# Attention and a three-way maxout layer on one core: raw weights decoded three in a row in the middle of a visit

## The chip, the cores and the metric

One core of a Trainium2 chip runs the whole program. The metric is the time of one execution on the device in microseconds, as the median of several runs.

## The reference, cut to what matters

```python
# q, k, v: (8, 12, 448, 64) float32
scores = q @ k.T / sqrt(64) - log(448)
attn   = 1 / (1 + exp(-scores))
x      = (attn @ v), heads side by side        # 3584 tokens x 768
h      = max(x @ w1, x @ w2, x @ w3)           # each weight 768 x 768
out    = h @ w_out                             # 768 x 768
```

The weights reach the kernel as the bits of float64 numbers, two 32-bit words each, and the kernel turns them into float32 itself: that is a "decoding".

## The kernel before, in words

Every product of two float32 matrices is made of three matmuls on a high and a low part of each operand (`hi` is the operand rounded, `lo` is what is left: ScalarE copies `hi`, VectorE subtracts). The attention part takes the first 246 us. Behind it come twelve visits: three stages of four visits, one for each pair of batches, and a stage is one block of output columns. In a visit a 2x2 block product by Winograd's scheme needs seven block products (`PRODUCTS`) for each of the three weights: 21 products of nine matmuls. In the texts they are counted @0 to @20: @0 to @6 are w1 (q = 0), @7 to @13 w2, @14 to @20 w3. Then the last layer runs 15 steps for each of the four pairs (`STEPS`, two output halves a step, six matmuls each).

Order: every instruction is pinned, so each engine and SP's DMA queue run in program order, and a wait holds all that stands behind it. The order inside a visit is: the product's matmuls; what takes its result; the copies and subtractions for the next visit's tokens (`his`, `los`, mostly at @14 to @20 and at the first products of the next visit); the splits of the next stage's weights (`ws`); weight loads (`w_loads`); then a decoding, if the list `decodes` names this place.

What takes the results: the first product of a weight goes to PSUM bank 0, and ScalarE copies it (`p1`, L807); the second goes to bank 1 and VectorE adds `p1` (`u2`, L810); the third to bank 3, VectorE adds `u2` (`u3`, L813); the fourth to bank 2, and `put("22")` adds `u3` (L786 for w1, L791 and the maximum L792 for w2 and w3). The fifth goes on in bank 0, the sixth takes a new buffer of bank 1, the seventh goes on in bank 2 after `put("22")` has read it (`put("12")`). Banks 2 and 3 have one buffer, 0 and 1 have two.

A decoding (`decode`, L203 to L225) is two ScalarE activations (L210, L211) and four VectorE instructions (L212 to L221) on a tile `wb`, of which there is one. Stage weights are then stored to DRAM (L238); the last layer's go into tiles `wd0` to `wd2`, and after every third `l_sums` puts fifteen sums of them into the tile `sums` on GpSimd (L264), with stores that follow over the next twelve products. The generator loads `ahead` raw tiles (`wraw`): at a decoding it first issues the load of the tile `ahead - 1` further on, then decodes, then stores.

Other users of the queues: at the head of a visit `x_load_all` issues seven loads of the next visit's tokens on SP (stages 1 and 2); in stage 0 the tokens are loaded at @4 and GpSimd forms their sums (L314, twelve instructions). `w_load` loads four blocks of the next stage's weights (L178) and GpSimd forms four sums (L173). In the last visit (`plan`, `EARLY`) the last layer's first operands are loaded (`l_load`), summed on GpSimd (`l_sum`, L648), copied (`l_hi`, L662, with a second copy into PSUM at L665) and subtracted (`l_lo`, L672), and its weights are split likewise (`wl_split`, L686 and L688; `wl_lo`, L695). All PSUM copies share one pair of banks (`ps_av`).

Of the kernel before, what the change touches and what calls it, by code (L numbers as in the profile page):

```python
# [8 lines left out]
F32 = mybir.dt.float32  # L9
F32R = mybir.dt.float32r  # L10
# [3 lines left out]
ALU = mybir.AluOpType  # L14
# [3 lines left out]
P = 128  # L18
# [21 lines left out]
L_SUMS = (  # L40
    ("n9", "a6", "+", "a7"),
    ("w3", "a1", "-", "n9"),
    ("w8", "w3", "-", "a8"),
    ("n12", "a5", "+", "w8"),
    ("w10", "a2", "+", "n12"),
    ("n16", "a4", "+", "a8"),
    ("w6", "n9", "+", "n16"),
    ("w9", "a5", "-", "a6"),
# [48 lines left out]
def attention_then_maxout(  # L97
# [9 lines left out]
    nc = tc.nc  # L107
    B, NK = qk.shape[0], qk.shape[1]
    S = qk.shape[3] // 2
    T = B * S  # L110
    C = S // P
    HALF = NK // 2
# [3 lines left out]
    pin = tc.keep_in_program_order  # L116
# [21 lines left out]
    xo_p = [pool(ctx, "xo", 1)]  # L138
# [111 lines left out]
    wl, wl_p, w_work = [], [], []  # L250
# [89 lines left out]
    FIRST = [x for _, x, _ in PRODUCTS[:2]]  # L340
# [239 lines left out]
    c_p = pool(ctx, "c", 2, reuse_waits="tile")  # L580
    dec_p = pool(ctx, "dec2", 1, reuse_waits="tile")
# [18 lines left out]
    his, los, ws, w_loads = {}, {}, {}, {}  # L600

    for n in range(1, done):
        (st0, p0), (st, p) = visits[n - 1], visits[n]
        if st != st0:
            when = [[(n - 1, 1, k // 2) for k in range(7)],
                    [(n - 1, 2, 2 + k // 2) for k in range(7)],
                    [(n, 0, 3 + k // 2) for k in range(6)] + [(n, 1, 0)]]
            for q in range(3):
                for key, (name, _, _) in zip(when[q], PRODUCTS):
                    ws.setdefault(key, []).append((q, name))  # L610
            w_loads[n - 2, 0, 0] = st, 0
            w_loads[when[0][-1]] = st, 1
            w_loads[when[1][-1]] = st, 2
        if p != p0:
            for k, (_, name, _) in enumerate(PRODUCTS):
                his[n - 1, 2, k] = name
            keys = [(n - 1, 2, k) for k in range(1, 5)] + [(n, 0, k) for k in (0, 2, 3)]
            for key, (_, name, _) in zip(keys, PRODUCTS):
                los[key] = name
# [5 lines left out]
    BEFORE = 3 * len(PRODUCTS)  # L625
    slots = ["xs_b11", "xs_t2", "xs_b12", "xs_t1", "xs_b21", "xs_t4", "xs_b22"]
    SETS = ("b11", "t2", "t3", "t1")
    l_raw, l_ops, l_px, wl_ops = {}, {}, {}, {}
# [26 lines left out]

    def l_hi(v, s):
        g, x = v * len(STEPS) + s, l_raw[v, STEPS[s][1]][0]
        name = SETS[g % len(SETS)]
        to = xo_p[name not in FIRST]
        hi = to.tile([P, HALF, S], F32R, name=f"xhi_{name}")  # L660
        lo = to.tile([P, HALF, S], F32R, name=f"xlo_{name}")
        pin(nc.scalar.copy(out=hi[:, :2], in_=x))  # L662
        if room(v, s):
            px = ps_av.tile([P, 2, 512], F32, name="ps_av")
            pin(nc.scalar.copy(out=px[:, :, :S], in_=x))  # L665
            x = px[:, :, :S]
        l_ops[g], l_px[g] = (hi, lo), x

    def l_lo(v, s):
        g = v * len(STEPS) + s  # L670
        hi, lo = l_ops[g]
        pin(nc.vector.tensor_tensor(  # L672
            out=lo[:, :2], in0=l_px.pop(g), in1=hi[:, :2].bitcast(F32), op=ALU.subtract
        ))

    def wl_load(j):
# [23 lines left out]
    for v in pairs:  # L700
# [6 lines left out]

    EARLY = {
        (l_load, "b3"): 4, (l_load, "b1"): 4, (l_load, "b2"): 5, (l_load, "b0"): 6,
        (l_load, "b5"): 7, (l_load, "b4"): 16,  # L710
        (l_sum, "s7"): 8, (l_sum, "s2"): 9, (l_sum, "s3"): 10, (l_sum, "s0"): 12,
        (l_sum, "s6"): 19, (l_sum, "s15"): 20,
        (l_hi, 0): 16, (l_hi, 1): 18, (l_hi, 2): 19, (l_hi, 3): 20,
        (l_lo, 0): 17, (l_lo, 1): 19, (l_lo, 2): 20, (l_lo, 3): 21,
    }

    def place(v, s, _, run, what, *rest):
# [20 lines left out]
    for j in range(2 * len(STEPS) * 2 // HALF):  # L738
        plan.setdefault(j + 1, []).append(lambda j=j: wl_load(j))
    for at, *tiles in (  # L740
        *((2 * k + 5, 2 * k, 2 * k + 1) for k in range(7)),
        (BEFORE, 14, 15), (BEFORE + 1, 16), (BEFORE + 4, 17), (BEFORE + 6, 18), (BEFORE + 7, 19),
    ):
        made = []
        plan.setdefault(at, []).append(lambda made=made, tiles=tiles: made.extend(wl_split(*tiles)))
        plan.setdefault(at + 1, []).insert(0, lambda made=made: wl_lo(*made))

    def l_plan(at):
# [1 line left out]
            run()  # L750

    decodes = {
        0: (8, 14), 1: (6, 10, 14), 2: (6, 10, 14), 3: (10,), 4: (0, 6, 10, 13), 5: (10, 13),
        6: (4, 10, 13), 8: (0, 10, 13), 9: (4, 10, 13), 10: (4,),
    }
    decodes = [(n, *divmod(at, len(PRODUCTS))) for n in decodes for at in decodes[n]]
    todo = [(1, 2, 3)] + [(2, q, n) for q in range(3) for n in range(4)]
    todo += [(STAGES, u, n) for u in range(2) for n in range(2 * HALF)]
    background = decoding(dec_p, todo, 1, 2, c_p)


    x_first = xs
# [107 lines left out]
    def l_out(q, name):  # L870
        to, tag, bufs = {
            "c": ((c_p, "p1", 1), (c_p, "u2", 1)),
            "t": ((m_p, "m11", 1), (m_p, "m22", 1)),
            "u": ((m_p, "m12", 1), (m_p, "m21", 1)),
            "d": ((c_p, "u3", 1), (c_p, "c", 2)),
            "e": ((wl_p[0], "e", 1), (c_p, "c", 2)),
        }[name][q]
        return to.tile([P, S], F32, name=tag, bufs=bufs)

# [90 lines left out]
```

## Time and profile before

| | |
|---|---|
| median of 3 runs | 868.73 us (867.54 to 872.42) |
| the profiled execution | 871.16 us, span from first to last instruction 869.3 us |
| TensorE busy | 850.3 us, 98% |
| VectorE, ScalarE, GpSimd busy | 77%, 55%, 26% |
| HBM | 113.31 MB read, 52.69 MB written |
| busy DMA queues | hardware ones, q1 with 165.92 of 166.95 MB |

A row of the timeline has the start and the length in us, the engine, the line, the operation and its operands; a bracket says how long the engine stood idle before it and what released it. Busy shares are averages over stages with different limits.

### The profile page before, as it was taken

The page shows a single profiled execution, that of the slowest core. Times are in us where ns is not written, and L with a number is a line of the kernel's source. Part 1 is how long each engine was busy: PE and PEld are TensorE (multiplying, and loading weights), DVE is VectorE, ACT ScalarE, POOL GpSimd, SP SyncE. Part 2 cuts the span into 40 slices and gives each one's busy share as a digit, 9 for nine tenths or more (in the row PEclk, how much of TensorE's full clock was granted, in tenths as well). Part 3 has the DMA queues.
Part 4 walks back from the last instruction along what each step waited for, and adds up shares of the span by engine and source line. Part 5 has one row for each costly group of instructions (what it writes and reads, how often), then busy time and mean ns, then how long its engine had stood idle before and what let it go on. Part 6 is the DMA issues. An engine that isn't in the chain of part 4 may idle for free.

```text
span 869.3 us, 14523 instructions
## 1 busy us (share of the span) xinstructions
PE 850.3 (98%) x5410; PEld 701.6 (81%) x5410; DVE 669.5 (77%) x928; ACT 479.2 (55%) x654; POOL 230.3 (26%) x192
## 2 busy tenths in 40 slices
PE   9999999999999999999899989999999998999998
PEld 5555555555579989899799978999989997999997
DVE  5677668876888897977586768769595778897895
ACT  6888888888864251423243333135152468777774
POOL 0010020202115436212000050250303227677660
PEclk9999999999999999999999999999999999999999
DMA  8667776776684656524643741292834643645423
GB/s 290 206 208 242 250 252 231 259 278 227 207 305 186 203 197 230 206 61 170 230 168 146 269 132 43 71 348 81 304 133 177 224 131 125 206 139 206 139 74 127
DMA packets 79878, 166.95 MB, mean 192 GB/s; under 512 B 7616, under 2 KB 55744, under 8 KB 79808
## 3 DMA queue, kind: packets, MB, share of 16 engines
q1 hardware_dynamic: 79664, 165.92, 54.9%
q8 instruction: 42, 0.69, 0.3%
q14 instruction: 28, 0.23, 0.1%
q10 hardware_dynamic: 144, 0.11, 0.0%
HBM read 113.31 MB, written 52.69 MB: 191 GB/s over the span
## 4 chain that ended last, share of the span: by engine, by line
PE 85%; DVE 4%; DMA 4%; issue 3%; POOL 2%; SPq 1%; ACT 0%; DVEq 0%; POOLq 0%; ACTq 0%
PE ps_y L591 42%; PE ps_y L860 16%; PE ps_s L430 9%; PE ps_s L454 7%; PE ps_av L454 6%; PE ps_s L465 2%; PE ps_s L443 2%; PE ps_av L430 2%; DMA wraw<-w 1%; DMA ws_a<-w_dram 1%; DVE c L791 1%; POOL sums L264 1%; DVE wb L216 1%; DVE wb L220 1%; DVE wb L212 0%
## 5 line engine op out<-in xcount | busy, mean ns | idle before, releaser
L400 ACT ACTIVATE a<-ps_s,bias_s 128x896 f32<-128x896 f32 x121 | 114.7, 1017 | 10.8 <-PE ps_s L430 10.7
L591 PE MATMUL ps_y<-xhi_t,wlo_s 128*128 128x448 f32 x324 | 117.3, 362 | 2.9 <-DVE c L791 2.9
L591 PE MATMUL ps_y<-xhi_t,whi_s 128*128 128x448 f32 x324 | 117.4, 362 | 0.0
L591 PE MATMUL ps_y<-xlo_t,whi_s 128*128 128x448 f32 x324 | 117.3, 362 | 0.0
L173 POOL TENSOR_TENSOR ws_s<-ws_a,ws_a 128x384 f32<-128x384 f32 x9 | 10.0, 1116 | 312.3 <-DMA ws_a<-w_dram 206.5
L807 ACT COPY p<-ps_y 128x448 f32<-128x448 f32 x36 | 19.1, 532 | 125.2 <-PE ps_y L591 104.3
L591 PE MATMUL ps_y<-xhi_b,wlo_a 128*128 128x448 f32 x216 | 78.6, 364 | 2.8 <-ACT p L807 2.8
L591 PE MATMUL ps_y<-xhi_b,whi_a 128*128 128x448 f32 x216 | 78.7, 364 | 0.0
L591 PE MATMUL ps_y<-xlo_b,whi_a 128*128 128x448 f32 x216 | 78.5, 363 | 0.0
L210 ACT ACTIVATE c<-wraw 128x384 f32<-128x384 f32 x48 | 27.5, 572 | 74.1 <-DVE m L792 38.3
L591 PEld LDWEIGHTS ps_y<-xhi_t,wlo_s 128*128 128x128 f32 x324 | 60.7, 187 | 7.5 <-DVE c L791 3.5
L591 PEld LDWEIGHTS ps_y<-xlo_t,whi_s 128*128 128x128 f32 x324 | 60.8, 188 | 4.3
L591 PEld LDWEIGHTS ps_y<-xhi_t,whi_s 128*128 128x128 f32 x324 | 60.8, 188 | 3.8
L454 PE MATMUL ps_av<-a,v 64*64 64x448 f32 x576 | 62.6, 536 | 0.0
L454 PE MATMUL ps_s<-a,v 64*64 64x448 f32 x576 | 59.7, 544 | 0.0
L791 DVE TENSOR_TENSOR c<-ps_y,u 128x448 f32<-128x448 f32 x72 | 44.5, 619 | 14.7 <-PE ps_y L591 14.4
L412 DVE TENSOR_TENSOR lo<-qk,hi 128x896 fp32r<-128x896 f32 (+4 forms) x51 | 53.5, 1049 | 1.8
L792 DVE TENSOR_TENSOR m<-c,m 128x448 f32<-128x448 f32 x72 | 52.8, 733 | 2.5
L454 PEld LDWEIGHTS ps_av<-a,v 64*64 64x64 f32 x576 | 22.0, 133 | 32.1 <-issue 32.1
L430 PE MATMUL ps_s<-hi 64*128 64x448 f32 x240 | 47.0, 388 | 0.0
L349 DVE TENSOR_TENSOR xlo_b<-xs_b,xhi_b 128x1344 fp32r<-128x1344 f32 x30 | 46.8, 1560 | 0.0
L349 DVE TENSOR_TENSOR xlo_t<-xs_t,xhi_t 128x1344 fp32r<-128x1344 f32 x30 | 46.5, 1549 | 0.0
(204 smaller groups left out, 2229.6 us busy)
## 6 DMA issues: line engine op xcount, KB each, us to landing
qk<-qk SPq DMA_DIRECT2D x47, 448.0 KB, 4.7
xs_b<-x_dram SPq DMA_DIRECT2D x30, 672.0 KB, 7.6
wraw<-w SPq DMA_DIRECT2D x36, 384.0 KB, 5.4
xs_t<-t_dram SPq DMA_DIRECT2D x18, 672.0 KB, 8.1
v<-v SPq DMA_DIRECT2D x24, 448.0 KB, 5.7
h_dram<-m SPq DMA_DIRECT2D x48, 224.0 KB, 1.9
x_dram<-m SPq DMA_DIRECT2D x47, 224.0 KB, 3.0
t_dram<-xs_t SPq DMA_DIRECT2D x12, 672.0 KB, 4.6
```

What stands on the lines that cost most here:

```text
L210: pin(nc.scalar.activation(out=square, in_=high.bitcast(F32), func=AF.Square))
L349: pin(nc.vector.tensor_tensor(out=lo, in0=x, in1=hi.bitcast(F32), op=ALU.subtract))
L400: pin(nc.scalar.activation(out=a, in_=banks[:, :, :S], func=AF.Sigmoid, bias=bias_s, scale=scale))
L412: pin(nc.vector.tensor_tensor(out=lo[:, cols], in0=t[:, cols], in1=high.bitcast(F32), op=ALU.subtract))
L430: pin(nc.tensor.matmul(bank[e][:, :S], kt[r, S + c * P : S + (c + 1) * P], qt[r, :S], start=n == 0, stop=n == len(terms) - 1,))
L443: pin(nc.tensor.matmul(ps[g * D : (g + 1) * D, e, :S], t[r, S + C * P :], t[r, :S], start=True, stop=True,))
L454: pin(nc.tensor.matmul(ps[e * D : (e + 1) * D, :S], vt[rows, (g * C + c) * 2 + e], chunks[c][rows, e], start=c == 0 and not (ahead and r = ...
L591: pin(nc.tensor.matmul(ps[:, :S], wt[:, k * P : (k + 1) * P], xt[:, k], start=first and n == 0, stop=n == len(terms) - 1, skip_group_check ...
L791: pin(nc.vector.tensor_tensor(out=c, in0=y, in1=add, op=ALU.add))
L792: pin(nc.vector.tensor_tensor(out=m[name], in0=c, in1=m[name], op=ALU.max))
L807: pin(nc.scalar.copy(out=p1, in_=ps[0][:, :S]))
L860: pin(nc.tensor.matmul(ps[:, :S], wl_ops[j][part][:, c * P : (c + 1) * P], xt[:, k], start=first and m == 0, stop=m == len(terms) - 1, ski ...
```

## The change: what it does

The places of the decodings move (`decodes`): from up to four in a visit, at places from @0 to @14, to mostly three in a visit at @4, @6 and @8. `ahead` goes from 2 to 3. The first weight load of the last stage moves from visit 6 @0 to @9. In the last visit the first operand of the last layer gets its high and low part in the tile `sums`, so that it can be split at @11 and not @16; the next three go to the sets of tiles that come free, at @15, @17 and @19; the sums and the weight splits move accordingly, and two more weight splits are done singly, without the copy into PSUM. For the space, the tile `e` goes (its place is `sums`), and a scratch area is halved.

```diff
--- before.py
+++ after.py
@@ -608,7 +608,7 @@
             for q in range(3):
                 for key, (name, _, _) in zip(when[q], PRODUCTS):
                     ws.setdefault(key, []).append((q, name))
-            w_loads[n - 2, 0, 0] = st, 0
+            w_loads[(n - 2, 0, 0) if st == 1 else (n - 2, 1, 2)] = st, 0
             w_loads[when[0][-1]] = st, 1
             w_loads[when[1][-1]] = st, 2
         if p != p0:
@@ -655,11 +655,19 @@
 
     def l_hi(v, s):
         g, x = v * len(STEPS) + s, l_raw[v, STEPS[s][1]][0]
-        name = SETS[g % len(SETS)]
-        to = xo_p[name not in FIRST]
-        hi = to.tile([P, HALF, S], F32R, name=f"xhi_{name}")
-        lo = to.tile([P, HALF, S], F32R, name=f"xlo_{name}")
-        pin(nc.scalar.copy(out=hi[:, :2], in_=x))
+        if g:
+            name = SETS[(g - 1) % len(SETS)]
+            to = xo_p[name not in FIRST]
+            hi, lo = (
+                to.tile([P, HALF, S], F32R, name=f"x{part}_{name}")[:, :2] for part in ("hi", "lo")
+            )
+        else:
+            both = wl_p[0].tile([P, len(L_SUMS) * P], F32R, name="sums")
+            hi, lo = (
+                both[:, k * 2 * S : (k + 1) * 2 * S].rearrange("p (a s) -> p a s", a=2)
+                for k in range(2)
+            )
+        pin(nc.scalar.copy(out=hi, in_=x))
         if room(v, s):
             px = ps_av.tile([P, 2, 512], F32, name="ps_av")
             pin(nc.scalar.copy(out=px[:, :, :S], in_=x))
@@ -670,7 +678,7 @@
         g = v * len(STEPS) + s
         hi, lo = l_ops[g]
         pin(nc.vector.tensor_tensor(
-            out=lo[:, :2], in0=l_px.pop(g), in1=hi[:, :2].bitcast(F32), op=ALU.subtract
+            out=lo, in0=l_px.pop(g), in1=hi.bitcast(F32), op=ALU.subtract
         ))
 
     def wl_load(j):
@@ -707,11 +715,11 @@
 
     EARLY = {
         (l_load, "b3"): 4, (l_load, "b1"): 4, (l_load, "b2"): 5, (l_load, "b0"): 6,
-        (l_load, "b5"): 7, (l_load, "b4"): 16,
-        (l_sum, "s7"): 8, (l_sum, "s2"): 9, (l_sum, "s3"): 10, (l_sum, "s0"): 12,
-        (l_sum, "s6"): 19, (l_sum, "s15"): 20,
-        (l_hi, 0): 16, (l_hi, 1): 18, (l_hi, 2): 19, (l_hi, 3): 20,
-        (l_lo, 0): 17, (l_lo, 1): 19, (l_lo, 2): 20, (l_lo, 3): 21,
+        (l_load, "b5"): 7, (l_load, "b4"): 12,
+        (l_sum, "s7"): 8, (l_sum, "s0"): 9, (l_sum, "s2"): 10, (l_sum, "s3"): 11,
+        (l_sum, "s6"): 17, (l_sum, "s15"): 19,
+        (l_hi, 0): 11, (l_hi, 1): 15, (l_hi, 2): 17, (l_hi, 3): 19,
+        (l_lo, 0): 12, (l_lo, 1): 16, (l_lo, 2): 18, (l_lo, 3): 20,
     }
 
     def place(v, s, _, run, what, *rest):
@@ -738,8 +746,9 @@
     for j in range(2 * len(STEPS) * 2 // HALF):
         plan.setdefault(j + 1, []).append(lambda j=j: wl_load(j))
     for at, *tiles in (
-        *((2 * k + 5, 2 * k, 2 * k + 1) for k in range(7)),
-        (BEFORE, 14, 15), (BEFORE + 1, 16), (BEFORE + 4, 17), (BEFORE + 6, 18), (BEFORE + 7, 19),
+        *((at, 2 * k, 2 * k + 1) for k, at in enumerate((5, 7, 9, 12, 14, 16, 18))),
+        (BEFORE + 1, 14), (BEFORE + 4, 15), (BEFORE + 6, 16), (BEFORE + 7, 17), (BEFORE + 8, 18),
+        (BEFORE + 9, 19),
     ):
         made = []
         plan.setdefault(at, []).append(lambda made=made, tiles=tiles: made.extend(wl_split(*tiles)))
@@ -750,13 +759,13 @@
             run()
 
     decodes = {
-        0: (8, 14), 1: (6, 10, 14), 2: (6, 10, 14), 3: (10,), 4: (0, 6, 10, 13), 5: (10, 13),
-        6: (4, 10, 13), 8: (0, 10, 13), 9: (4, 10, 13), 10: (4,),
+        0: (8,), 1: (6, 9), 2: (8,), 3: (4, 6, 8), 4: (0, 5, 8), 5: (4, 6, 8),
+        6: (4, 6, 8), 8: (4, 6, 8), 9: (4, 6, 8), 10: (4, 6, 8),
     }
     decodes = [(n, *divmod(at, len(PRODUCTS))) for n in decodes for at in decodes[n]]
     todo = [(1, 2, 3)] + [(2, q, n) for q in range(3) for n in range(4)]
     todo += [(STAGES, u, n) for u in range(2) for n in range(2 * HALF)]
-    background = decoding(dec_p, todo, 1, 2, c_p)
+    background = decoding(dec_p, todo, 1, 3, c_p)
 
 
     x_first = xs
@@ -873,7 +882,7 @@
             "t": ((m_p, "m11", 1), (m_p, "m22", 1)),
             "u": ((m_p, "m12", 1), (m_p, "m21", 1)),
             "d": ((c_p, "u3", 1), (c_p, "c", 2)),
-            "e": ((wl_p[0], "e", 1), (c_p, "c", 2)),
+            "e": ((wl_p[0], "sums", 1), (c_p, "c", 2)),
         }[name][q]
         return to.tile([P, S], F32, name=tag, bufs=bufs)
 
@@ -956,7 +965,7 @@
         "wout": by_tiles(moe_w_out),
     }
     nc = bacc.Bacc(
-        "TRN2", target_bir_lowering=False, num_devices=1, dynamic_dma_scratch_size=2048
+        "TRN2", target_bir_lowering=False, num_devices=1, dynamic_dma_scratch_size=1024
     )
     args = [
         nc.dram_tensor(name, a.shape, mybir.dt.from_np(a.dtype), kind="ExternalInput").ap()
```

## Rows read from the trace of the kernel before

**Rows 1.** The page: busy time by engine; one of the costliest groups.

```profile
PE 850.3 (98%) x5410; PEld 701.6 (81%) x5410; DVE 669.5 (77%) x928; ACT 479.2 (55%) x654; POOL 230.3 (26%) x192
...
L791 DVE TENSOR_TENSOR c<-ps_y,u 128x448 f32<-128x448 f32 x72 | 44.5, 619 | 14.7 <-PE ps_y L591 14.4
```

**Rows 2.** Timeline of TensorE from 246 us on, the matmuls that waited.

```profile
320.90 0.47 PE L591 MATMUL ps_y<-xhi_b,wlo_s 128*128 128x448 f32 x1 [0.97 <-DVE c L791]
...
361.29 0.57 PE L591 MATMUL ps_y<-xhi_b,wlo_s 128*128 128x448 f32 x1 [1.97 <-DVE c L791]
...
425.32 0.47 PE L591 MATMUL ps_y<-xhi_b,wlo_a 128*128 128x448 f32 x1 [2.76 <-ACT p L807]
...
516.46 0.47 PE L591 MATMUL ps_y<-xhi_t,wlo_s 128*128 128x448 f32 x1 [2.87 <-DVE c L791]
...
523.86 0.47 PE L591 MATMUL ps_y<-xhi_b,wlo_s 128*128 128x448 f32 x1 [1.72 <-DVE c L791]
...
638.34 0.47 PE L591 MATMUL ps_y<-xhi_b,wlo_s 128*128 128x448 f32 x1 [0.79 <-DVE c L791]
...
718.93 0.47 PE L860 MATMUL ps_y<-xlo_t,whi_s 128*128 128x448 f32 x1 [0.31 <-DVE xlo_t L672]
...
726.37 0.47 PE L860 MATMUL ps_y<-xhi_t,wlo_a 128*128 128x448 f32 x1 [2.52 <-DVE p L903]
```

**Rows 3.** Span and mean granted TensorE clock of the core.

```profile
core 0: 869.3 us, clock 0.994
```

**Rows 4.** Windows behind two waits: length, busy us (count) by engine, clock, DMA share, GB/s.

```profile
361.30:364.80 3.50, 3.50 (x10) 3.13 (x11) 3.50 (x4) 0.00 (x0) 0.00 (x0) 0.53 0.21 75
...
516.50:520.50 4.00, 4.00 (x20) 3.75 (x21) 3.74 (x7) 4.00 (x5) 0.00 (x0) 1.00 0.51 153
```

**Rows 5.** Timeline of VectorE and GpSimd in visit 1, decodings among token sums.

```profile
300.59 1.40 DVE L221 SCALAR_TENSOR_TENSOR wb<-c,wb 128x384 f32<-128x384 f32 x1
...
305.64 1.31 DVE L212 TENSOR_SCALAR wb<-wraw 128x384 uint32<-128x384 uint32 x1
...
306.70 4.13 POOL L314 TENSOR_TENSOR xs_t<-xs_b,xs_t 128x448 f32<-128x448 f32 x3
...
309.85 1.40 DVE L221 SCALAR_TENSOR_TENSOR wb<-c,wb 128x384 f32<-128x384 f32 x1
```

**Rows 6.** Timeline of SP's queue and VectorE in visit 4, first two decodings.

```profile
413.49 1.19 SPq L238 DMA_DIRECT2D w_dram<-wb  x1
...
424.33 0.36 DVE L212 TENSOR_SCALAR wb<-wraw 128x384 uint32<-128x384 uint32 x1 [8.32 <-DMA w_dram<-wb]
...
426.02 0.56 DVE L221 SCALAR_TENSOR_TENSOR wb<-c,wb 128x384 f32<-128x384 f32 x1
```

**Rows 7.** Tile wb from 400 to 432 us: its three stores, issue to landing.

```profile
DMA to landing us min/median/max: 1.8/1.9/10.8
```

**Rows 8.** Windows of visit 5, columns as in rows 4 (last but one: DMA share).

```profile
460.00:463.00 3.00, 3.00 (x16) 2.81 (x16) 0.63 (x1) 1.04 (x3) 0.00 (x0) 1.00 1.02 392
463.00:466.00 3.00, 3.00 (x16) 2.81 (x16) 1.56 (x3) 0.00 (x0) 0.00 (x0) 1.00 0.11 45
```

**Rows 9.** Timeline of GpSimd and VectorE in visit 6.

```profile
502.95 1.02 POOL L173 TENSOR_TENSOR ws_s<-ws_a,ws_a 128x384 f32<-128x384 f32 x1 [91.98 <-DMA ws_a<-w_dram]
...
513.28 0.56 DVE L221 SCALAR_TENSOR_TENSOR wd<-c,wb 128x384 f32<-128x384 f32 x1 [5.15 <-POOL sums L264]
```

**Rows 10.** Timeline of ScalarE and VectorE in visits 8 and 9.

```profile
584.28 0.55 ACT L210 ACTIVATE c<-wraw 128x384 f32<-128x384 f32 x1 [5.11 <-DMA wraw<-wout]
...
621.19 0.55 ACT L210 ACTIVATE c<-wraw 128x384 f32<-128x384 f32 x1 [4.68 <-DMA wraw<-wout]
...
628.06 0.56 DVE L221 SCALAR_TENSOR_TENSOR wd<-c,wb 128x384 f32<-128x384 f32 x1 [3.84 <-DMA wl_dram<-wd]
```

**Rows 11.** Timeline of ScalarE at the start of the last layer.

```profile
718.90 0.91 ACT L665 COPY ps_av<-xs_b 128x896 f32<-128x896 f32 x1 [1.75 <-DVE xlo_t L672]
...
724.67 0.52 ACT L899 COPY p<-ps_y 128x448 f32<-128x448 f32 x1
```

## The prediction

> **What bounds the kernel now.** The page comes first: TensorE is busy 98% of the span [rows 1], so nothing can be won but the 2% in which it stands still or runs slowly. The timeline of TensorE alone shows where that is: after the attention part there are eight waits worth naming [rows 2]. Seven of them end on VectorE, one on ScalarE. Each costs its bracket and about 0.27 us more until the beat is back (320.90: start-to-start 0.31 instead of 0.20 behind it, and 0.16 ahead). So the waits cost 1.24 us in visit 1, 2.24 in visit 2, 3.03 in visit 4, 3.14 and 1.99 in visit 6, 1.06 in visit 9, 0.58 and 2.79 at the start of the last layer: 16.1 us. The third cost is the clock: its mean over the span is 0.994, so 0.006 of 869.3 or 5.2 us are lost [rows 3]. The windows show how: behind the wait that ends at 361.29 ten matmuls need 3.5 us (granted 0.53, the 1.2 GHz level), behind the longer one that ends at 516.46 twenty need 4.0 us at 1.00 (2.4 GHz) [rows 4]. Ten matmuls at the lower level cost about 1.75 us, so 5.2 us is three such spells: some three of the five waits above 1.7 us lost the clock, and the length of the wait does not say which. At most 21 us can come back.
>
> At full clock a matmul takes 0.20 us, a product of nine 1.80, a visit of 21 products 37.8. I count products of a visit from @0 to @20; the due start of any product follows from a row of [rows 2], less its wait. One dependence decides nearly everything: bank 2 has one PSUM buffer. Products @3, @10, @17 fill it, VectorE's addition (put "22") reads it, and three products later @6, @13, @20 go on in it. So VectorE may be 3.6 us late with put "22", and then TensorE stands.
>
> **The change, part by part.** The work of a decoding is unchanged: two ScalarE and four VectorE instructions, 25 times. Only the places move, and a place has a price. With GpSimd idle the four VectorE instructions take 424.33 to 426.58, 2.2 us [rows 6]; with GpSimd's token sums running, 305.64 to 311.25, 5.6 us [rows 5].
>
> *Visits 1 and 2.* Before, decodings at @6, @10, @14 pushed the splits of the next visit's tokens late, and @20 waited. Visit 2 keeps one, at @8. It stands in GpSimd's sums and begins when product @8 (end due at 339.3) is added up, about 340.1; at 5.6 us and two PSUM additions of 0.62 [rows 1] put "22" is done at 347.1. @13 is due at 346.5, so 0.7 us at most; visit 0 has the same decoding in the same place and no wait in the list. I take 0.3 us instead of 2.24. Visit 1 has @6 and now @9, which is ahead of put "22" in VectorE's order (@10 was behind it). The @6 decoding ends at 302.0 [rows 5]; its store must land before the next may write the single tile wb, 1.9 us later (the median of [rows 7]), 304.0; plus 5.6 is 309.6, and put "22" is done at 310.3. @13 is due at 307.2: 3.2 us with the restart, against 1.24.
>
> The Trainium skill ("SBUF — State Buffer", section "SBUF: two separate sides") says that VectorE and GpSimd lock their shared port pair for a whole instruction. By that, four instructions would each wait out one of GpSimd's 1.38 us, and a decoding would take 7.8 us, visit 1's stall 5.4; the rows give 5.6 us, and these decide.
>
> *Visit 3* gets three (@4, @6, @8), 2.2 us each, GpSimd idle. Put "22" of @10 then ends about 0.7 us before @13 is due. Nothing.
>
> *Visit 4.* The raw weights three ahead take away ScalarE's wait for them, which held the copy that @11 needed (3.03 us). But the second decoding moves from @6 to @5. The store of the first (@0) stands in SP's queue behind seven token loads (128x1344 float32 each), is issued at 413.49 and lands 10.8 us later, at 424.3; that is when VectorE's next decoding could write wb, after 8.32 us of standing idle [rows 6, 7]. Nothing in the change moves that store. At @6 the wait stood behind put "12"; at @5 it stands ahead of it, and @10 needs put "12" to have emptied bank 2. @10 is due at 420.6 (1.80 before @11's 422.4). It would start at 424.3 + 2.2 + 0.6 + 0.1 = 427.2: 6.7 us with the restart, against 3.03. Between nothing and this I take this, since a row shows the very wait.
>
> *Visit 5* had two decodings without a store and no stall. Now @4, @6, @8 each store. The first ends about 457.0 (product @4 ends at 454.0, then one ScalarE copy and two activations of about 0.55, two VectorE instructions). Its store goes behind the token loads, which keep the DMA engines full until 463 [rows 8]: it lands about 463.8. @6 runs to 466.0, its store lands at 468.0, @8 runs to 470.2, then two additions: put "22" at 471.5. @13 is due at 468.4 (25 products before visit 6's @17): 3.2 us. If the store is as quick as the median [rows 7], zero.
>
> *Visit 6.* The four loads of the next stage's weights stood ahead of the last layer's sums in GpSimd's queue: GpSimd sat until 502.95, so the sums came late, and VectorE's write of a tile that they read waited 5.15 us [rows 9]. Both stalls hang on this, 5.1 us. Loading after @9 puts the sums first, and three decodings per visit give the tiles a visit to come free. Both go. The loads land some ten products before their first reader, so being late costs nothing. *Visit 9's* 1.06 us goes likewise: its VectorE wait was for stores of such a tile, 3.84 us [rows 10].
>
> *The third raw tile of a row* is what is late next. A decoding first loads the tile two further on, so the third of a row is loaded at @4 behind the token loads. Such loads landed at 584.28 (visit 8, 20.7 us after its start) and 621.19 (visit 9, 19.8) [rows 10]. Landing, then 2.2 us and two additions: 587.8 in visit 8 against 587.0 due, 0.9 us with the restart; 624.7 in visit 9 against 624.8. For visits 6, 9 and 10 together 0.3.
>
> *Last layer.* ScalarE and VectorE pass one PSUM pair to and fro for the splits; ScalarE stood 1.75 us on VectorE at 718.90 and copied step 0's result only at 724.67 [rows 11]. Step 3's bank waited for what follows that copy. The first operand's split goes to @11 (into the sums tile, idle by then), the other three to @15, @17, @19 with one pair of weight splits between each, so the hand-overs end about a product and a half into step 0, two steps before the copy is needed. I take 0.4 us for 3.4. Against it: two more weight splits are done singly.
>
> *At nothing:* tile e shares the sums tile (first written fifteen steps later), and the smaller scratch (the page's busy queues are hardware ones).
>
> **Sum.** Now: 1.24 + 2.24 + 3.03 + 5.13 + 1.06 + 3.37 = 16.1 us of waits, 5.2 of clock. Then: 3.2 + 0.3 + 6.7 + 3.2 + 0.3 + 0.9 + 0.4 = 15.0. Clock: visit 4's wait surely loses it, visits 1 and 5 three times in five: 1.75 x 2.2 = 3.9. Difference -2.4 us. The profiled execution took 871.16 us (span 869.3), the median of the runs shown is 868.73; I carry the difference over: 866.3 us. The stalls are moved more than removed.
>
> **Rivals.**
> *The stores do not hold TensorE* in visits 4 and 5. For: ScalarE's raw tile came at the same moment, and a wait for several things is put down to the last, so 8.32 us could be mostly the load's, which three ahead removes. Against: the store's own 10.8 us [rows 7]. Then 6.7, 3.2 and 2.8 of clock go: 853.6 us.
> *Slower: the third raw tile lands later.* Four visits (6, 8, 9, 10) each have it decoded ahead of put "22", with margins from 0.1 to -0.8 us. It decides from 19.9 us after a visit's start; each us beyond costs four. Two us later than the rows gives 874 us. For: the queue is full just then, and visit 4's store came 21.7 us after the start. Against: visits 8 and 9 show 20.7 and 19.8 with the same loads ahead.
> *The last layer keeps its stalls*: they are a chain of ping-pong that is respread, not shortened. Then 3.0 and 1.75 come back: 871 us.
>
> **Chances.** My forecast 0.48 (its own range 862 to 871), no hold by the stores 0.28, the last layer unchanged 0.12, the late third tile 0.12. 0.5% of 868.73 is 4.3 us, about what can be told from no change: faster means under 864.4, slower over 873.1. Faster gets all but a little of the second case and a third of the forecast, 0.45; slower two thirds of the late tile and the tails of the others, 0.15; the rest, 0.40, is the same. The range reaches from the store rival's 854 to 873.
>
> **What would show it.** Right: waits on VectorE ending about 310.3 (@13 of visit 1), at @10 of visit 4 near 6.5 us behind an idle VectorE that a w_dram store releases, at @13 of visit 5; none in visit 6 and 9, and none at step 3 of the last layer. Wrong: visit 4 without a wait, or with a store that lands early; waits at @13 in visits 6, 9, 10 on raw loads; ScalarE still late at the first steps. A different number of clock drops shifts the time by 1.75 us each.

## The result, and the profile after

| | before | after |
|---|---|---|
| median of 9 runs each, on the same chip | 868.73 us (865.61 to 872.42) | 875.59 us (873.62 to 877.65) |
| the profiled execution | 871.16 us, span 869.3 us | 874.99 us, span 873.2 us |

The changed kernel takes 1.0075 times as long (95% interval 1.0052 to 1.0098): slower, by more than the 0.5% that count here, and 9.3 us over the forecast of 866.3. Of the 6.9 us between the medians the two traces show 3.9 (the spans). The rest lies mostly in the profiled execution of before, 2.4 us above its median. A likely reason is the granted clock, 0.994 in that execution [rows 3]: among the runs of before that stood beside the experiments below, those granted 0.994 took 868.8 to 872.2 us and those granted 0.998 took 866.4 to 869.6, and 0.002 to 0.004 of 869 us is 1.7 to 3.5 us.

The core, and the page's busy times after: as before [rows 1] to 1.1 us, but for GpSimd, which is 6 us busier.

```profile
core 0: 873.2 us, clock 0.994
```

```profile
PE 850.9 (97%) x5410; PEld 700.5 (80%) x5410; DVE 670.0 (77%) x928; ACT 479.7 (55%) x652; POOL 236.4 (27%) x192
```

The timeline of TensorE from 246 us on, the matmuls that waited; it answers to [rows 2].

```profile
269.45 0.48 PE L591 MATMUL ps_y<-xhi_b,wlo_s 128*128 128x448 f32 x1 [0.18 <-DVE c L800]
...
308.71 0.48 PE L591 MATMUL ps_y<-xhi_b,wlo_s 128*128 128x448 f32 x1 [1.18 <-DVE c L800]
...
347.12 0.47 PE L591 MATMUL ps_y<-xhi_b,wlo_s 128*128 128x448 f32 x1 [0.34 <-DVE c L800]
...
423.41 0.74 PE L591 MATMUL ps_y<-xhi_t,wlo_s 128*128 128x448 f32 x1 [5.80 <-DVE m L795]
...
472.67 0.48 PE L591 MATMUL ps_y<-xhi_b,wlo_s 128*128 128x448 f32 x1 [3.21 <-DVE c L800]
...
588.70 0.47 PE L591 MATMUL ps_y<-xhi_b,wlo_s 128*128 128x448 f32 x1 [0.53 <-DVE c L800]
...
627.57 0.47 PE L591 MATMUL ps_y<-xhi_b,wlo_s 128*128 128x448 f32 x1 [0.79 <-DVE c L800]
...
666.41 0.47 PE L591 MATMUL ps_y<-xhi_b,wlo_s 128*128 128x448 f32 x1 [0.77 <-DVE c L800]
...
737.33 0.47 PE L869 MATMUL ps_y<-xlo_t,whi_s 128*128 128x448 f32 x1 [0.95 <-DVE xlo_t L680]
...
743.54 0.44 PE L869 MATMUL ps_y<-xhi_b,wlo_a 128*128 128x448 f32 x1 [1.10 <-DVE m L912]
...
746.52 0.45 PE L869 MATMUL ps_y<-xhi_t,wlo_s 128*128 128x448 f32 x1 [0.33 <-DVE p L912]
...
751.08 0.44 PE L869 MATMUL ps_y<-xhi_t,wlo_a 128*128 128x448 f32 x1 [1.91 <-DVE m L912]
```

All twelve end on VectorE. In the visits they stand at @13 (L800 is put "22") and once, longest of all, at @10 of visit 4 (L795 is put "12" of w1). The last four are in the last layer. None stands in visit 6, and none at step 3 of the last layer, where before had that layer's largest.

To compare, the loss of a stretch is its length less what it would take without a stop: a visit 37.8 us from its first matmul to the next visit's, a step of the last layer 2.40 us. This takes waits, restarts and clock together:

| loss, us | v0 | v1 | v2 | v3 | v4 | v5 | v6 | v7 | v8 | v9 | v10 | v11 | visits | steps 0 to 11 |
|---|---|---|---|---|---|---|---|---|---|---|---|---|---|---|
| before | 0.1 | 1.3 | 4.0 | 0.1 | 4.6 | 0 | 5.2 | 0 | 0 | 1.1 | 0 | 0 | 16.4 | 5.1 |
| after | 0.6 | 1.5 | 0.6 | 0 | 8.7 | 5.1 | 0.2 | 0 | 0.8 | 1.1 | 1.1 | 0 | 19.5 | 6.0 |

3.1 us more in the visits and 0.9 in the last layer make 4.0; the first visit starts 0.25 us sooner, and 3.8 is how much later the last matmul starts.

Each row is one execution, and executions of one kernel differ: the nine of after lie 4.0 us apart. So a loss of a few tenths says little. Visit 8 loses between 0 and 1.5 us in the traces of after, e1, e3, e4, e7 and e8, which all have the same order in it, and visit 2 loses 0.6 us in after and nothing in those five.

**Visits.** VectorE in visits 1, 4, 5 and 9 (timeline):

```profile
302.71 1.13 DVE L212 TENSOR_SCALAR wb<-wraw 128x384 uint32<-128x384 uint32 x1
...
306.73 1.39 DVE L221 SCALAR_TENSOR_TENSOR wb<-c,wb 128x384 f32<-128x384 f32 x1
...
420.58 0.36 DVE L212 TENSOR_SCALAR wb<-wraw 128x384 uint32<-128x384 uint32 x1 [8.47 <-DMA w_dram<-wb]
...
464.89 0.36 DVE L212 TENSOR_SCALAR wb<-wraw 128x384 uint32<-128x384 uint32 x1 [5.57 <-DMA w_dram<-wb]
...
623.94 0.36 DVE L212 TENSOR_SCALAR wb<-wraw 128x384 uint32<-128x384 uint32 x1 [3.63 <-DMA wraw<-wout]
```

Tile wb from 400 to 432 us, its stores from issue to landing, as in [rows 7]:

```profile
DMA to landing us min/median/max: 1.8/1.9/12.3
```

In visits 4 and 5 the second decoding stands idle until the first one's store has landed, 8.47 and 5.57 us. That store took 12.3 us in visit 4 and 7.0 in visit 5, the other stores of these two visits 1.8 to 1.9. In visit 9, which starts at 603.2, the third raw tile lands at 623.9, 20.7 us later; in visits 6, 8 and 10 it lands 20.0, 20.5 and 20.7 us after the start.

**Clock and last layer.** Windows of after, columns as in [rows 4]: behind the waits of visits 4 and 5, then the first steps of the last layer.

```profile
423.40:427.40 4.00, 3.99 (x11) 3.57 (x12) 3.43 (x7) 0.00 (x0) 0.00 (x0) 0.50 0.52 147
427.40:431.40 4.00, 4.00 (x18) 3.69 (x17) 1.98 (x4) 0.00 (x0) 0.00 (x0) 0.80 0.13 49
...
474.60:476.60 2.00, 2.00 (x7) 1.78 (x6) 1.09 (x3) 0.00 (x0) 0.00 (x0) 0.50 0.00 0
...
719.00:735.00 16.00, 15.86 (x79) 14.39 (x78) 15.57 (x17) 14.33 (x23) 14.89 (x7) 1.00 0.54 186
735.00:757.00 22.00, 17.71 (x84) 15.02 (x84) 20.92 (x23) 12.29 (x18) 12.64 (x6) 1.00 0.33 109
```

Windows of before, the same steps (its last layer starts at 715.85, that of after at 718.73):

```profile
716.00:735.00 19.00, 16.17 (x72) 14.18 (x71) 15.14 (x18) 15.54 (x25) 15.37 (x8) 0.91 0.50 164
735.00:757.00 22.00, 22.00 (x112) 20.46 (x111) 21.15 (x27) 16.73 (x22) 12.71 (x7) 1.00 0.49 168
```

The third busy figure is VectorE's: in the first window 15.57 of 16 us after, where before had 15.14 of 19, and 20.92 of 22 in the second. VectorE is full, and before's two waits at steps 1 and 3 have become four at steps 7 to 11. (A wait is counted at the step whose matmuls stand.) What fills VectorE (timeline of VectorE and GpSimd, after):

```profile
720.70 0.55 DVE L703 TENSOR_TENSOR wlo_a<-ps_av,whi_a 128x384 fp32r<-128x384 f32 x1
...
725.23 2.13 POOL L648 TENSOR_TENSOR xlo_b<-xs_b,xs_t 128x896 f32<-128x896 f32 x1
...
725.69 2.09 DVE L703 TENSOR_TENSOR wlo_a<-wlo_a,whi_a 128x384 fp32r<-128x384 f32 x1 [0.36 <-ACT whi_a L694]
...
729.72 2.98 POOL L648 TENSOR_TENSOR xlo_b<-xlo_b,xs_t 128x896 f32<-128x896 f32 x1
...
730.63 3.02 DVE L680 TENSOR_TENSOR xlo_t<-xs_t,xhi_t 128x896 fp32r<-128x896 f32 x1
...
739.31 2.14 POOL L648 TENSOR_TENSOR xs_t<-xhi_b,xs_b 128x896 f32<-128x896 f32 x1 [1.08 <-issue]
...
740.16 1.71 DVE L703 TENSOR_TENSOR wlo_s<-wlo_s,whi_s 128x384 fp32r<-128x384 f32 x1
...
744.29 0.56 DVE L703 TENSOR_TENSOR wlo_s<-wlo_s,whi_s 128x384 fp32r<-128x384 f32 x1 [0.36 <-ACT whi_s L694]
```

A weight split that reads its raw value from PSUM takes 0.55 us; done singly, in place, 2.09 and 1.71 us, and 0.56 where GpSimd stands idle (it has nothing between 741.45 and 746.87). The six single splits of after take 2.09, 1.63, 1.71, 0.56, 2.14 and 0.56 us: 8.7 us, against 4.3 for before's four.

The splits are only half of it. Four of the tokens' subtractions (L680) are done in place as well, in before as in after. In after all four run beside GpSimd's sums and take 2.01, 3.02, 1.98 and 2.06 us, 9.1 in all; in before three of the four find GpSimd idle and take 1.08 us, only one 2.05, 5.3 in all. So over these steps VectorE has 4.4 us more of splits and 3.8 us more of subtractions whose number and form did not change.

### The profile page after: what moved, and what is told of

It is laid out like the page before. It is cut to its first block, busy times and chain, and to the rows that moved or that the text cites. A ratio compares the mean times of both kernels' runs of the same rounds, so it can differ in the third digit from the quotient of the medians.

```text
span 873.2 us, 14553 instructions
## 1 busy us (share of the span) xinstructions
PE 850.9 (97%) x5410; PEld 700.5 (80%) x5410; DVE 670.0 (77%) x928; ACT 479.7 (55%) x652; POOL 236.4 (27%) x192
## 5 line engine op out<-in xcount | busy, mean ns | idle before, releaser
L264 POOL TENSOR_TENSOR sums<-wd 128x128 f32<-128x128 f32 x16 | 7.2, 462 | 179.9 <-DVE wd L221 179.9
L800 DVE TENSOR_TENSOR c<-ps_y,u 128x448 f32<-128x448 f32 x72 | 44.5, 618 | 7.9 <-PE ps_y L591 7.0
L819 DVE TENSOR_TENSOR u<-ps_y,p 128x448 f32<-128x448 f32 x36 | 22.4, 623 | 33.4 <-PE ps_y L591 25.0
```

Of the source, the lines that this page charges most:

```text
L800: pin(nc.vector.tensor_tensor(out=c, in0=y, in1=add, op=ALU.add))
L819: pin(nc.vector.tensor_tensor(out=u2, in0=ps[1][:, :S], in1=p1, op=ALU.add))
```

## The experiments

Each starts from the changed kernel (e9 and e10 from e6) and was timed beside the kernel before on the same chip: one chip for e1 to e4, one for e5 to e8, one for e9 and e10. So the ratios, not the medians, are what compares across groups. Losses are worked out as above, from one trace of each.

| | edit | median, us | before beside it | ratio, 95% interval | visits | steps 0 to 11 |
|---|---|---|---|---|---|---|
| e1 | stores from three tiles in turn | 861.97 | 869.14 | 0.9908 [0.9880, 0.9936] | 5.0 | 6.1 |
| e2 | places of before | 868.27 | 869.14 | 0.9988 [0.9971, 1.0005] | 9.9 | 7.2 |
| e3 | splits 14, 15 as a pair | 871.69 | 869.14 | 1.0027 [1.0009, 1.0045] | 20.5 | 4.0 |
| e4 | all splits as pairs | 870.82 | 869.14 | 1.0013 [0.9998, 1.0029] | 18.5 | 2.9 |
| e5 | third decoding at @10 | 866.4 | 868.39 | 0.998 [0.9966, 0.9993] | 7.9 | 9.1 |
| e6 | e1, e4 and e5 together | 853.75 | 868.39 | 0.9822 [0.9804, 0.9839] | 0.1 | 3.9 |
| e7 | last layer's places of before | 872.38 | 868.39 | 1.0045 [1.0026, 1.0064] | 19.6 | 5.3 |
| e8 | early weight load of before | 879.18 | 868.39 | 1.0122 [1.0100, 1.0144] | 20.4 | 7.1 |
| e9 | e6, raw weights two ahead | 880.49 | 869.11 | 1.0131 [1.0105, 1.0156] | 24.9 | 3.4 |
| e10 | e6, first pair two products later | 852.65 | 869.11 | 0.9819 [0.9801, 0.9837] | 0.2 | 3.4 |

**e1: do the stores hold TensorE?** The decodings that are stored to DRAM write wd0, wd1 and wd2 in turn, which lie idle in that stage, so that none waits for a store.

```diff
...
+                bits = None
+                if wl_p:
+                    bits = wl_p[0].tile([P, HP], F32, name=f"wd{k % HALF}").bitcast(U32)
-                pin(nc.sync.dma_start(out=w_dram[st, q][:, n], in_=decode(raws[k], None)))
+                pin(nc.sync.dma_start(out=w_dram[st, q][:, n], in_=decode(raws[k], None, bits)))
```

> The stage decodings of the visits write the three tiles wd0 to wd2 in turn (idle until visit 6) in place of the single wb, so a store has two further decodings' time to land. All else is the changed kernel. Theory (the landing of the store holds VectorE in visits 4 and 5): the wait of 5.80 us at @10 of visit 4 goes, and what is left is the third raw tile, which lands about 21 us after the visit's start and holds put 22 to about 24.7 us against 23.4 due: visit 4's loss falls from 8.65 us to about 1.4, visit 5's from 5.09 to under 1. Together about 11 us, so some 864 us. Rival (VectorE waits there for raw weights or for the full queue in general, the store only lands at the same moment): the waits stay within 1 us, 875 us.

Visit 4 loses 1.2 us and not 8.7, visit 5 nothing and not 5.1; the median falls by 13.6 us (the ratio to before from 1.0075 to 0.9908). What is left in visit 4 is the third raw tile (timeline of VectorE):

```profile
419.31 0.36 DVE L213 TENSOR_SCALAR wd<-wraw 128x384 uint32<-128x384 uint32 x1 [3.91 <-DMA wraw<-w]
```

The stores into a single tile are shown to be what holds these two visits.

**e2: the places alone.** The list `decodes` of before, all else of after.

```diff
-        0: (8,), 1: (6, 9), 2: (8,), 3: (4, 6, 8), 4: (0, 5, 8), 5: (4, 6, 8),
-        6: (4, 6, 8), 8: (4, 6, 8), 9: (4, 6, 8), 10: (4, 6, 8),
+        0: (8, 14), 1: (6, 10, 14), 2: (6, 10, 14), 3: (10,), 4: (0, 6, 10, 13), 5: (10, 13),
+        6: (4, 10, 13), 8: (0, 10, 13), 9: (4, 10, 13), 10: (4,),
```

> The changed kernel with the list of decoding places of before; three raw tiles ahead, the late weight load and the new start of the last layer stay. Theory (the places of the decodings cost the time): visits 1 and 2 lose again what they lost before (1.3 and 4.0 us), visit 4 about 3 to 4 (the raw tile is early, but the store still holds the second decoding, now behind put 12), visits 5, 6, 8 and 10 next to nothing, visit 9 about 1: some 11 us in place of 19.5, about 867 us. Rival (three ahead, by the order of the transfers, or the late load costs it): the time stays at 875 us.

The visits lose 9.9 us, 9.6 less than in after, and the ratio falls from 1.0075 to 0.9988, some 7.6 us: the new places cost that. Against before no difference of the times is shown (the interval holds 1). In the traces the visits lose 6.5 us less than in before, but 1.6 us of this is the clock in visit 2, lost behind before's wait of 1.97 us and not behind e2's of 1.92, and e2's last layer loses 2.1 us more than before's. What three ahead and the later load are worth at the old places is therefore not shown in the time.

The expectation was wrong on visit 6: next to nothing was forecast and 3.3 us are lost, in waits of 1.04 us at @17 and 1.72 at @20, although the weight load is late. There VectorE's write of a tile `wd`, at 507.23, stands idle 3.98 us for a store of that tile (`wl_dram`).

**e3 and e4: the single splits.** e3 makes 14 and 15 one pair again, e4 makes three pairs of the six.

The edit of e4:

```diff
-        (BEFORE + 1, 14), (BEFORE + 4, 15), (BEFORE + 6, 16), (BEFORE + 7, 17), (BEFORE + 8, 18),
-        (BEFORE + 9, 19),
+        (BEFORE, 14, 15), (BEFORE + 3, 16, 17), (BEFORE + 5, 18, 19),
```

> The changed kernel with the single weight splits of before: 14 and 15 again as one pair through PSUM, four singles in place of six. Theory (VectorE is full from step 3 to step 11 of the last layer, and an in-place split beside GpSimd takes 1.6 to 2.1 us in place of 0.55): VectorE has some 1.6 us less to do there for each of the two, and the loss in the first eleven steps falls from 6.0 to about 3 us. Rival (the chain of hand-overs over the one PSUM pair sets it): the loss stays at 5 to 6 us, since a pair adds a hand-over.

> As before this one, but all six of the last weight splits go in pairs through PSUM (at steps 0, 3 and 5), none in place. Theory (in-place splits fill VectorE): its time for splits falls from 8.7 us to 3.3, and the loss in the first eleven steps to about 1 us, 5 us less in all, about 870 us. Rival (hand-overs over the one PSUM pair): the loss stays at 5 us or grows.

The first twelve steps lose 4.0 and 2.9 us and not 6.0. The single splits are a cause, but not the whole: with all in pairs, 1.3 us are left at step 3 and again at step 7 (timeline of TensorE, e4):

```profile
726.56 0.47 PE L868 MATMUL ps_y<-xhi_t,wlo_a 128*128 128x448 f32 x1 [1.18 <-DVE p L911]
...
737.63 0.47 PE L868 MATMUL ps_y<-xhi_t,wlo_s 128*128 128x448 f32 x1 [1.19 <-ACT u L907]
```

Ahead of the first, ScalarE stands 1.21 us on a subtraction of VectorE for the PSUM pair and copies step 0's result late, as in before [rows 11], so part of the loss moved back to the hand-overs. In e4 the four token subtractions in place take 1.08 to 1.15 us each: with the singles gone they start where GpSimd is idle or about to end a sum. So e4 takes away both parts of VectorE's extra work, and how much each of them is worth is not separated.

**e5: the third decoding behind put "22".** It goes from @8 (@9 in visit 1) to @10; visit 3 keeps @8.

```diff
-        0: (8,), 1: (6, 9), 2: (8,), 3: (4, 6, 8), 4: (0, 5, 8), 5: (4, 6, 8),
-        6: (4, 6, 8), 8: (4, 6, 8), 9: (4, 6, 8), 10: (4, 6, 8),
+        0: (10,), 1: (6, 10), 2: (10,), 3: (4, 6, 8), 4: (0, 5, 10), 5: (4, 6, 10),
+        6: (4, 6, 10), 8: (4, 6, 10), 9: (4, 6, 10), 10: (4, 6, 10),
```

> The changed kernel with its last decoding of a visit at @10 and not at @8 (@9 in visit 1, @8 in visits 0 and 2), so that it stands behind put 22; the single wb stays. Theory (the third raw tile lands some 21 us after the visit's start and holds put 22): the losses of visits 8, 9 and 10 (0.82, 1.06, 1.05 us) go; those of visits 0 to 2 (0.57, 1.45, 0.62) go too, since the decoding among the token sums then stands behind put 22. Visit 5's 5.09 falls below 1, since its second decoding ends about 21 us after the start and only the third waits for a store. Visit 4 keeps its 8.65, as the decoding at @5 stays. About 9 us less, 866 us. Rival (a decoding anywhere in the middle costs VectorE as much, the wait only moves to @17 or @20): no visit but visit 5 changes by more than half, 871 us or more.

Visits 0 to 2, 5 and 8 to 10 lose 0.2 us at most. For visits 1, 9 and 10 this is the edit: 1.4 to 1.5, 0.5 to 1.1 and 0.7 to 1.1 us are lost in after, e1, e3, e4, e7 and e8. For visit 5 too: the single tile stays, and 5.1 us become 0.2, so the store costs only where the third decoding stands ahead of put "22". Visits 0, 2 and 8 lose next to nothing in some of those traces without it, so for them it is not shown. Visit 4 still loses 7.4 us, behind its first store (timeline of VectorE):

```profile
416.80 0.36 DVE L212 TENSOR_SCALAR wb<-wraw 128x384 uint32<-128x384 uint32 x1 [7.86 <-DMA w_dram<-wb]
```

The last layer, whose order is untouched, loses 9.1 us here, 3.1 more than in after; e2 and e8 show 7.2 and 7.1. The four waits at steps 7 to 11 have the same lengths, to 0.01 us, in after, e1, e2, e5 and e8. What differs is the clock behind the last of them, 1.91 or 1.92 us long: from 751 to 757 us in after it is 1.00, from 740.3 to 744.4 in e5 0.60, from 753 to 756 in e8 0.50. This costs e5 1.6 us, and a wait at step 4 that is short in after makes most of the rest (timeline of TensorE, e5):

```profile
718.10 0.47 PE L869 MATMUL ps_y<-xlo_t,whi_a 128*128 128x448 f32 x1 [1.11 <-DVE xlo_t L680]
...
740.35 0.44 PE L869 MATMUL ps_y<-xhi_t,wlo_a 128*128 128x448 f32 x1 [1.91 <-DVE m L912]
```

**e6: the three together.** e1, e4 and e5 in one kernel.

> The three edits together: stage decodings write wd0 to wd2 in turn, last decoding of a visit at @10, all last weight splits in pairs through PSUM. If the causes are separate, the visits lose about 1 us in all and the last layer 3: 8 us less than the first experiment, about 854 us. If VectorE's backlog only moves on, it shows as waits at @17, @20 or later steps, and the time stays near 860 us.

853.75 us, 1.8% below before; the visits lose 0.1 us in all. One wait is left, at step 3 (timeline of ScalarE and TensorE):

```profile
705.89 0.48 ACT L700 COPY ps_av<-wlo_a 128x384 f32<-128x384 f32 x1 [1.20 <-DVE xlo_t L684]
...
707.13 0.52 ACT L911 COPY p<-ps_y 128x448 f32<-128x448 f32 x1
...
708.84 0.47 PE L872 MATMUL ps_y<-xhi_t,wlo_a 128*128 128x448 f32 x1 [2.03 <-DVE p L915]
```

It is before's chain again [rows 11]: ScalarE stands on VectorE for the PSUM pair, copies step 0's result late, and step 3 waits.

**e7: the last layer's part undone.** `EARLY` and the places of the splits as in before; the first operand keeps its place in `sums`.

```diff
...
-        (l_hi, 0): 11, (l_hi, 1): 15, (l_hi, 2): 17, (l_hi, 3): 19,
-        (l_lo, 0): 12, (l_lo, 1): 16, (l_lo, 2): 18, (l_lo, 3): 20,
+        (l_hi, 0): 16, (l_hi, 1): 18, (l_hi, 2): 19, (l_hi, 3): 20,
+        (l_lo, 0): 17, (l_lo, 1): 19, (l_lo, 2): 20, (l_lo, 3): 21,
...
```

> The changed kernel with the places of the last layer's first loads, sums, copies and weight splits of before (the first operand still in the sums tile). Theory (spreading them out only moved the waits from steps 1 to 3 to steps 4 to 11, the work on VectorE is not less): the loss in the first twelve steps is 4 to 6 us and lies at steps 1 to 3 again, the time 873 to 876 us. Rival (the new places are a loss by themselves, since the pause at step 3 let VectorE catch up for nothing): the loss falls to 3 us or less.

The steps lose 5.3 us, now at 1 to 3 as in before, against 6.0 at 4 to 11. Of the 5.3, about 1.4 are the clock behind the wait at step 3 (2.52 us, then granted 0.60); after's 6.0 hold none. So the part moves the loss and does not shrink it: in waits alone the new order loses some 2 us more. The ratios, 1.0045 and 1.0075, point the same way, with intervals that just overlap.

**e8: the early weight load back.**

```diff
-            w_loads[(n - 2, 0, 0) if st == 1 else (n - 2, 1, 2)] = st, 0
+            w_loads[n - 2, 0, 0] = st, 0
```

> The changed kernel with the last stage's first weight load back at @0 of visit 6. My forecast held that load to be the cause of visit 6's two waits (5.1 us). Theory now (the tile that VectorE writes comes free in time because the next three decodings are two visits later, wherever the load stands): visit 6 stays under 1 us, the time within 1 us of 875. Rival (GpSimd's sums, late behind the load, still hold VectorE, by the tile or by slowing it): visit 6 loses 2 to 5 us again.

Visit 6 loses 5.2 us again, so at the new places the later load is what keeps it free; at the old ones it does not (e2). But the way there is another than in before (timeline of GpSimd, VectorE, TensorE):

```profile
505.77 1.01 POOL L173 TENSOR_TENSOR ws_s<-ws_a,ws_a 128x384 f32<-128x384 f32 x1 [99.58 <-DMA ws_a<-w_dram]
...
507.63 0.47 DVE L212 TENSOR_SCALAR wb<-wraw 128x384 uint32<-128x384 uint32 x1 [4.86 <-DMA wraw<-wout]
508.13 1.26 DVE L216 SCALAR_TENSOR_TENSOR wb<-wraw,wb 128x384 uint32<-128x384 uint32 x1
...
512.57 0.47 PE L591 MATMUL ps_y<-xhi_b,wlo_s 128*128 128x448 f32 x1 [3.33 <-DVE c L800]
```

With four loads more ahead of it in the queue the third raw tile lands at 507.6, 22.0 us into the visit and not 20.0 as in after, and its decoding stands ahead of put "22". GpSimd's sums of the loaded weights, which started at 505.77, run beside it, and it takes 3.6 us and not 2.2. The two make 3.4 us; TensorE waits 3.33. In before VectorE's last instruction of a decoding waited for GpSimd's sums [rows 9]; here it does not, so of the rival it is the slowing that holds.

**e9: is three ahead needed?** From e6.

```diff
-    background = decoding(dec_p, todo, 1, 3, c_p)
+    background = decoding(dec_p, todo, 1, 2, c_p)
```

> The kernel of e6, but raw weights are loaded two ahead and not three. Theory (the landing of the raw tile decides): with two ahead the second tile of a visit is loaded at the visit's first decoding (@4, in visit 4 @0), behind the seven token loads, and so lands where the third landed in the kernel after, 20 to 21 us after the visit's start. Its decoding stands at @6, ahead of put 12 of w1, which @10 needs at 18.0 us. Landing, then 2.2 us and one addition of 0.6: @10 starts near 24 us, so about 5 to 6 us in each of visits 4, 5, 6, 8, 9 and 10, some 30 us: 880 to 890 us, slower than before. Rival (the load of a single raw tile slips between the token loads, and three ahead is worth little): under 1 us a visit, 854 to 858 us.

880.49 us, 26.7 over e6: visits 4, 9 and 10 lose 8.0, 6.9 and 5.8 us, 6 and 8 1.8 and 2.0, 5 only 0.3. The theory holds in its direction and its sum, not evenly by visit. Timeline of VectorE, ScalarE and TensorE in visits 4 and 9:

```profile
417.30 0.36 DVE L213 TENSOR_SCALAR wd<-wraw 128x384 uint32<-128x384 uint32 x1 [8.38 <-DMA wraw<-w]
...
420.13 0.74 PE L595 MATMUL ps_y<-xhi_t,wlo_s 128*128 128x448 f32 x1 [5.72 <-DVE m L798]
...
620.79 0.55 ACT L211 ACTIVATE c<-wraw 128x384 f32<-128x384 f32 x1 [12.85 <-DMA wraw<-wout]
...
622.27 0.54 PE L595 MATMUL ps_y<-xhi_b,wlo_a 128*128 128x448 f32 x1 [5.00 <-ACT p L819]
```

Set beside e1 and after, visit 4 tells most. After loads early and stores from one tile: the store holds, TensorE waits 5.80 us. e9 has no store to wait for, but a late load: the raw tile holds, 5.72 us. e6 has neither, and no wait. In before both lay on one place: ScalarE got the second raw tile at 423.86 (below), VectorE the store at 424.33 [rows 6], and a bracket names only the last to come.

```profile
423.86 0.55 ACT L210 ACTIVATE c<-wraw 128x384 f32<-128x384 f32 x1 [9.88 <-DMA wraw<-w]
```

**e10: the first pair later.** From e6.

```diff
-        (BEFORE, 14, 15), (BEFORE + 3, 16, 17), (BEFORE + 5, 18, 19),
+        (BEFORE + 2, 14, 15), (BEFORE + 3, 16, 17), (BEFORE + 5, 18, 19),
```

> The kernel of e6, but the first pair of the last weight splits (14, 15) goes two products of the last layer later. In e6 ScalarE copies step 0's result late, since its copy into the PSUM pair for the split stood 1.20 us on VectorE just ahead, and step 3 waited 2.03 us. Theory (this one hand-over holds the copy): the copy comes about 1.2 us earlier and step 3 does not wait; the last layer's first twelve steps lose 1 to 2 us and not 3.9, 851.5 us. Rival (the hand-overs are a chain that only moves): the wait turns up at a later step, 3.5 to 4.5 us lost, 853.5 us as e6.

Step 3 does not wait, but steps 4 and 7 do (timeline of TensorE):

```profile
709.80 0.47 PE L872 MATMUL ps_y<-xhi_t,wlo_a 128*128 128x448 f32 x1 [0.70 <-ACT m L911]
...
718.82 0.47 PE L872 MATMUL ps_y<-xhi_t,wlo_s 128*128 128x448 f32 x1 [1.39 <-ACT u L911]
```

3.4 us lost and not 3.9: nearer to the rival, the chain moves. 852.65 us is the shortest time of the study, but 1.1 us below e6 in another set of runs, with ratios of 0.9819 and 0.9822 to the kernel before, is no difference shown.

## Why the prediction was wrong

The sum put after at 15.0 us of waits and 3.9 of clock, 18.9; the trace has 25.6 (19.5 + 6.0). By its terms, with the clock beside the wait that lost it:

| term | forecast | measured |
|---|---|---|
| visit 1 | 3.2 + 1.05 | 1.5 |
| visits 2 and 0 | 0.3 + 0 | 0.6 + 0.6 |
| visit 4 | 6.7 + 1.75 | 8.7 |
| visit 5 | 3.2 + 1.05 | 5.1 |
| visits 6, 9, 10 | 0.3 | 0.2 + 1.1 + 1.1 |
| visit 8 | 0.9 | 0.8 |
| last layer | 0.4 | 6.0 |

**The step that failed: the last layer.** The prediction took "0.4 us for 3.4" because the hand-overs would end two steps before the copy is needed. That wait did go. But the work was only counted along that one chain, and not on VectorE, which the windows show 97% busy after (15.57 of 16 us). The objection was noted ("two more weight splits are done singly") and priced at nothing; the six singles took 8.7 us, 4.4 more than before's four, and the token subtractions, pushed beside GpSimd's sums, 3.8 us more. e7 shows that the old order loses about the same (5.3, clock included), e3 and e4 that without some or all of the singles 2 to 3 us of it go, and e4, e6 and e10 that pairs bring the hand-overs back. The rival "the last layer keeps its stalls" had the outcome, not the places. This term alone is 5.6 of the 6.7 us by which the sum was short; the other terms that were too small, 4.0 us together, are largely offset by visit 1, which was 2.8 too large.

The Trainium skill ("SBUF — State Buffer", section "SBUF: two separate sides") says that a VectorE instruction with two SBUF inputs contends with a GpSimd instruction that reads SBUF, that one with at most one SBUF input does not (VectorE's two-port modes set aside), and that whoever comes first holds the shared ports for its whole instruction. The trace agrees: 0.55 us from PSUM with GpSimd busy, 0.56 in place with GpSimd idle, 1.63 to 2.14 in place beside it. It agrees in detail, too. Each of the four slow splits ends 0.41 or 0.42 us after the GpSimd instruction that ran when it started (725.23 + 2.13 = 727.36, 725.69 + 2.09 = 727.78), whatever its own start, and each of the four slow token subtractions 0.94 to 0.96 us after. This rule was weighed for visit 1 and not for the last layer, where it spoke against the change.

For visit 1 it was worked out wrongly: its 7.8 us are four of GpSimd's 1.38 us on top of VectorE's own 2.2. In the rows the two engines take turns, and GpSimd's 1.38 us already hold VectorE's turn: three of these sums with VectorE idle take 3.39 us (after, at 259.14), 1.13 each. Four turns of 1.38 are 5.5 us, and the rows have 5.4 to 5.6.

**Third raw tile, mis-sized.** For visits 6, 9 and 10 the forecast was 0.3 us, from a landing 19.8 us after the start of visit 9 [rows 10]. It was 20.7 us there, as in visit 8 of before, 20.7 in visit 10 and 20.0 in visit 6; visits 9 and 10 lost 1.1 us each, visit 6 0.2. e5, which puts that decoding behind put "22", takes the loss of 9 and 10 away. That is the rival "the third raw tile lands later" just beyond the edge from which it decides (19.9 us).

**Right.** *Visit 4*: a wait at @10 behind a store, 6.1 us with the restart against 6.7, and 2.6 of clock against 1.75. *Visit 5*: at @13, 3.5 us with the restart against 3.2, and 1.6 of clock. e1 shows the cause of both and refutes "the stores do not hold TensorE". That visit 4's sum fits (8.7 against 8.45) is partly luck: the wait was taken 0.6 us too long and the clock 0.8 too cheap. *Visit 6* is free as forecast, by the later load (e8) together with the new places (e2 has the load and loses 3.3); the forecast had named both, but "both stalls hang on this", on GpSimd's late sums, was too much: in e2 the second stall is still 1.72 us. *Visit 8* loses 0.8 against 0.9, by luck as well, since it is 0 to 1.5 in other traces of the same order.

**Visit 1** was too dear: the decoding at @6 ran ahead of GpSimd's sums (VectorE starts it at 297.3, and it ends at 300.4 and not at 302.0), so only the second was slow, 302.71 to 308.12: 5.4 us against the 5.6 forecast.

**The size of the whole.** The prediction carried the difference of the profiled execution over to the median. On that scale it forecast 868.8 us, and the profiled execution of after took 874.99: 6.2 us off, about the 6.7 of the sum. The other 3.1 us are that before's profiled execution lay 2.4 us above its median and after's 0.6 below.

**Why the change made the kernel slower** is another question. At the new places the later load gains some 4 us (e8, ratios 1.0122 and 1.0075), and three raw tiles ahead instead of two gain 26.7 (e9 against e6). The last layer's part costs 0.9 us in the traces, or 0.7 against e7. The new places cost 9.6 us in the visits (e2), some 7.6 by the ratios, since three decodings close together meet one tile with a slow store and a third raw tile that lands just too late. With both mended (e6, e10) the change's other parts stand, and the kernel is 1.8% faster than before.

## What to carry to other kernels

Before a wait is taken away, list all that the waiting instruction depends on, and when each comes: in visit 4 the late load and the late store each cost 5.7 to 5.8 us alone, and only both mended gave the time back. When work is spread out in a stretch, add up the busy time of every engine in it, with each instruction at the duration of its new form and neighbours, since a chain that gets shorter can leave an engine full, and an instruction that nobody touched can slow down because it now meets another engine. Where the decoded data waits for a store, a second place to write it (here tiles that lay idle) was worth more than either other list of places tried (e1 against e2 and e5).

## What the runs showed of the hardware

A store of wb landed in 1.8 to 1.9 us, and in 12.3 us (visit 4 of after) or 7.0 (visit 5) when it was issued behind seven token loads of 672 KB and a raw load of 384 KB. In after's last layer the eight subtractions of VectorE with both inputs in SBUF that started during one of GpSimd's sums ended 0.41 us (128x384) or 0.95 us (128x896) after that sum, and not a fixed time after their own start. The clock did not follow the length of the wait alone: it went to 0.50 (the 1.2 GHz level) behind waits of 5.80 and 3.21 us (after), and step 3's 2.03 us in e6 cost 1.6 us more in the next step, but before's 2.87 us at 516.46 cost nothing beyond the wait and its restart [rows 4]. One and the same wait of 1.91 us, with the same three waits just ahead of it, lost the clock in e2, e5 and e8 and kept it in after and e1. Behind the 5.80 us it had not come fully back 4 us later (0.50, then 0.80), so this wait cost 2.6 us of clock where a spell of 1.75 was reckoned.
